# Early q and k on GpSimd's casting queue, a regrouped read of the tail tokens, and fixed operation lists in an attention and channel-mix kernel

## The chip, the core and the metric

The kernel runs on one core of a Trainium2 chip. A core has a matrix engine (TensorE, PE in the profile, with its weight loads as PEld), VectorE (DVE), ScalarE (ACT), GpSimd (POOL), SyncE (SP, which only issues transfers here), and 16 DMA engines that all queues share. SP and ACT have hardware queues (q1 and q10 in the profile); transfers that GpSimd issues go through a software queue (q0) and can change the type on the way. The metric is the time of one execution in microseconds.

## What is computed

`q`, `k` and `v` are [8 batches, 8 heads, 576 tokens, 64]. Everything is given and returned in fp32.

```python
scores = (q @ k^T) / 8 - slope[h] * |i - j|      # slope[h] = 2 ** -(h + 1)
scores where i - j is not in 0..127: -1e9        # causal, window of 128
x = softmax(scores) @ v                          # heads joined: [8, 576, 512]
xk = mu_k * x + (1 - mu_k) * x_prev              # x_prev: x of the token before
xr = mu_r * x + (1 - mu_r) * x_prev
out = sigmoid(xr @ w_r) * ((relu(xk @ w_k) ** 2) @ w_v)   # w_k 512x1024, w_v 1024x512
```

## The kernel before

Attention runs by batch and by pair of heads (g = 0 to 3). q and k are loaded with a cast to bf16, transposed so that the 64 dimensions of the two heads lie on the 128 partitions, and kept in `qk`; the last 64 tokens of a batch (`ts`, `tt`) go a way of their own. Scores of a pair are matmuls into a two-bank PSUM tile `duo` (L729), ACT takes the exponential (L743), VectorE multiplies with a mask that holds bias and window (L756; batch 0 adds the bias on TensorE instead, L716), and AV is a series of 65-column matmuls with a column of ones for the sum (L785). VectorE takes the reciprocal and scales the result into `xu` (L796), which is transposed into `xt`: on TensorE (L823 in batch 0, L840 in batches 1 to 5), or in batches 6 and 7 by a transposing DMA on SP's queue (`out_flip`). VectorE makes `dl` (x minus its predecessor, L883), `xk` and `xr` (L890).

The channel mix works on two batches together in chunks of up to 512 tokens: eight groups of four matmuls with w_k (L994), each followed by ACT's relu (L1001) and a square (L967) into `kk`; per 128 tokens one group of four with w_r (L1012) and ACT's tanh, and two groups of four with the two halves of w_v (L1028), whose sum VectorE multiplies with the gate into `ot` (L1033), which SP writes out. The first chunk of all takes the first 256 tokens of batch 0 (blocks c0 and c1), the second the next 256.

Batch 0 is cut in two parts: part 0 is tokens 0 to 255, part 1 the rest. Part 0's q and k come by hardware queues as fp32 (`first_load`, into `stage`): pairs 0 and 1 by one load each of q and k, cast by VectorE to bf16 and transposed with `ident`; pairs 2 and 3 (FT) by two loads each of q and k with 256 B runs, transposed as fp32 with `id32` in four 128x128 transposes a pair (L1133) and one copy. Part 1 comes by GpSimd's casting queue and is transposed by `qk_quad` in 64x64 blocks (L1089), as is batch 2's `wide_buf`. About 90 matmuls on a zero tile (L690) run whenever TensorE has nothing else at the start.

GpSimd issues its transfers in the order of `LOADS`; there v and V are the v loads of batch 0 (tokens 0 to 255, and the rest with the tail), K and k the halves of w_k, 2 and 3 part 1's q and k of heads 0 to 3 and 4 to 7, t the tail tokens of q and k, a, b and c batch 1's q and k, tail and v, R w_r, W and w the first and second half of w_v. Ahead of them GpSimd makes a distance tile (iota, L440) and cuts it to the window (two selects, L448 and L451).

A planner in Python (`Plan`) makes the order of each engine's instructions when the kernel is built. Each operation is added with its engines, an assumed duration and its dependencies; a simulation then picks, for each engine that is free, the ready operation with the lowest key. The key is the number in `PLACES` that belongs to the operation, with `pe_key` to keep 64-row and 128-row groups together on TensorE and `paced` to hold back transposes of later batches. On the chip each engine executes its list in order and waits by semaphores for data only.

```python
key = (n.place,) + tuple(n.prio)
if rows == 64 and n.rows[0] == 64:
    return (-1e8,) + tuple(key)
```

Of the kernel before, what the change touches and what calls it, by code (L numbers as in the profile page):

```python
# [21 lines left out]
PLACES = [int(x) for x in '''  # L22
# [71 lines left out]
class Plan:  # L94
# [6 lines left out]
    def __init__(self, sizes, pairs, wait=0.0):  # L101
        self.wait = wait
        self.nodes = []
        self.placed = 0
        self.free = {c: set(range(n)) for c, n in sizes.items()}
        self.pairs = pairs
# [1230 lines left out]
```

## Time and profile before

| | us |
|---|---|
| time, median of 3 runs | 232.08 (232.07 to 232.3) |
| time of the profiled execution | 232.05 |
| span of the profiled execution | 230.3 |
| PE busy | 223.5 (97%) |
| DVE busy | 187.7 (82%) |
| ACT busy | 163.1 (71%) |
| POOL busy | 93.9 (41%) |
| L690 warm-up matmuls, 0 to 14 us | 8.05 |

The span runs from the first instruction to the last; 1.75 us of the profiled execution lie around it. Busy time of TensorE is the time with at least one matmul in its pipeline, so 97% is not a share of its peak. GpSimd's busy time is mostly the writing of descriptors for its transfers. Of the 16 DMA engines' time, q0 takes 99.3%, q1 24.0% and q10 1.0% on the page, where several transfers may share an engine, so that shares over 100% occur.

### The profile page before, as it was taken

Reading aid. Unit: us, or ns where it says so; the run is one execution under the profiler, and the core shown is the slowest. Engines: PE = TensorE matmul, PEld = TensorE weight load, DVE = VectorE, ACT = ScalarE, POOL = GpSimd, SP = SyncE. Lnnn points to the kernel's source line nnn. Section 1 sums busy time; section 2 is a strip of 40 time slices with the busy share of each in tenths; the row PEclk is TensorE's granted clock in tenths of the full one; section 3 lists DMA queues with packets and bytes.
Section 4 is the critical chain, followed back from the end, with each engine's and each line's share of the span. In section 5 each row is a group of like instructions: output and inputs, shape, how many; then the busy total and the mean of one; then the engine's idle time right before and its main releaser. Section 6 shows DMA issues by size and latency. Waiting matters only on the chain.

```text
span 230.3 us, 6675 instructions
## 1 busy us (share of the span) xinstructions
PE 223.5 (97%) x2715; PEld 135.2 (59%) x2715; DVE 187.7 (82%) x423; ACT 163.1 (71%) x295; POOL 93.9 (41%) x120
## 2 busy tenths in 40 slices
PE   8999998999999999999999999999999999999994
PEld 8675764765656656455655745545765544545552
DVE  8496998799949998997678997999999979563252
ACT  3769999599989969999797747959476455117421
POOL 8787654579976960991004961700000000000000
PEclk9999999999999999999999999999999999999999
DMA  6999999999999999999643999995230330231032
GB/s 169 183 168 197 189 161 198 193 176 156 189 141 170 160 145 184 96 144 185 141 117 38 173 180 156 131 136 182 78 86 3 137 103 37 89 129 52 3 137 91
DMA packets 121566, 31.11 MB, mean 135 GB/s; under 512 B 108216, under 2 KB 117696, under 8 KB 121536
## 3 DMA queue, kind: packets, MB, share of 16 engines
q0 software_dynamic: 96016, 16.26, 99.3%
q1 hardware_dynamic: 23776, 13.84, 24.0%
q10 hardware_dynamic: 1744, 0.59, 1.0%
q8 instruction: 21, 0.34, 0.6%
q14 instruction: 9, 0.07, 0.1%
HBM read 33.56 MB, written 9.44 MB: 187 GB/s over the span
## 4 chain that ended last, share of the span: by engine, by line
PE 79%; DMA 12%; POOL 4%; issue 2%; DVE 1%; ACT 0%; DVEq 0%; POOLq 0%
PE uno L994 25%; PE uno L1028 25%; PE uno L1012 13%; PE duo L785 7%; PE duo L729 6%; DMA wv_sb<-in_moe_w_v_dram 5%; DMA cb<-in_k_dram 4%; DMA wk_sb<-in_moe_w_k_dram 3%; PE uno L840 3%; POOL vs L503 1%; POOL cb L499 1%; POOL tv L508 1%; DVE ot L1033 1%; PE uno L1089 1%; DVE xr L890 0%
## 5 line engine op out<-in xcount | busy, mean ns | idle before, releaser
L994 PE MATMUL uno<-xk,wk_sb 128*128 128x256 bf16 (+2 forms) x416 | 72.4, 314 | 0.7 <-ACT qk L699 0.4
L1028 PE MATMUL uno<-wv_sb,kk 128*128 128x512 bf16 (+2 forms) x296 | 69.3, 374 | 1.1 <-DMA wv_sb<-in_moe_w_v_dram 1.0
L743 ACT ACTIVATE at<-duo 128x1024 bf16<-128x1024 f32 (+2 forms) x68 | 65.0, 1002 | 5.9 <-PE duo L729 5.5
L1001 ACT ACTIVATE rl<-uno 128x256 bf16<-128x256 f32 (+2 forms) x104 | 48.3, 496 | 25.7 <-PE uno L994 25.1
L994 PEld LDWEIGHTS <-wk_sb 128*128 128x128 bf16 x416 | 38.6, 98 | 23.4 <-issue 0.8
L503 POOL DMA_DIRECT2D vs<-in_v_dram x32 | 28.5, 906 | 40.5 <-PE duo L785 33.7
L1028 PEld LDWEIGHTS <-kk 128*128 128x128 bf16 x296 | 27.2, 98 | 29.7 <-issue 1.5
L756 DVE TENSOR_TENSOR at<-at,mask 128x1024 bf16<-128x1024 bf16 x56 | 37.2, 681 | 7.2 <-ACT at L743 7.2
L967 DVE TENSOR_TENSOR kk<-rl 128x256 bf16<-128x256 bf16 (+2 forms) x96 | 31.3, 337 | 12.5 <-ACT rl L1001 12.0
L1019 ACT ACTIVATE rs<-uno 128x512 bf16<-128x512 f32 x36 | 22.1, 617 | 21.5 <-PE uno L1012 13.2
L1012 PE MATMUL uno<-wr_sb,xr 128*128 128x512 bf16 x144 | 36.9, 380 | 0.0
L1033 DVE SCALAR_TENSOR_TENSOR ot<-rs,uno 128x512 f32<-128x512 bf16 (+2 forms) x37 | 24.2, 662 | 10.7 <-PE uno L1028 8.6
L699 ACT COPY qk<-uno 128x512 bf16<-128x512 bf16 (+1 forms) x41 | 21.8, 600 | 4.7 <-PE uno L1089 3.2
L890 DVE SCALAR_TENSOR_TENSOR xr<-dl,mu_sb,xt 128x576 bf16<-128x576 bf16 (+1 forms) x32 | 24.5, 774 | 0.0
L890 DVE SCALAR_TENSOR_TENSOR xk<-dl,mu_sb,xt 128x576 bf16<-128x576 bf16 (+1 forms) x32 | 24.4, 772 | 0.0
L785 PEld LDWEIGHTS <-at 128*128 128x128 bf16 x576 | 21.2, 98 | 5.0 <-issue 0.4
L796 DVE TENSOR_TENSOR xu<-duo,rc 128x640 bf16<-128x640 f32 x28 | 22.8, 817 | 0.9 <-DMA xt<-xu 0.5
L1012 PEld LDWEIGHTS <-xr 128*128 128x128 bf16 x144 | 13.3, 98 | 13.0
L534 POOL DMA_DIRECT2D cb<-in_k_dram x20 | 17.9, 919 | 4.9 <-DMA vs<-in_v_dram 2.9
L785 PE MATMUL duo<-vs,at 128*128 128x65 bf16 x448 | 19.0, 194 | 0.0
L534 POOL DMA_DIRECT2D cb<-in_q_dram x20 | 17.7, 938 | 0.8 <-PE uno L840 0.7
L699 ACT COPY xt<-uno 128x512 bf16<-128x512 bf16 (+3 forms) x28 | 15.2, 580 | 2.5 <-PE uno L823 1.5
(83 smaller groups left out, 202.8 us busy)
## 6 DMA issues: line engine op xcount, KB each, us to landing
out_dram<-ot SPq DMA_DIRECT2D x30, 256.0 KB, 3.3
vs<-in_v_dram POOLq DMA_DIRECT2D x32, 128.0 KB, 6.6
cb<-in_q_dram POOLq DMA_DIRECT2D x20, 128.0 KB, 6.6
cb<-in_k_dram POOLq DMA_DIRECT2D x20, 128.0 KB, 5.9
out_dram<-ot SPq DMA_DIRECT2D x10, 128.0 KB, 1.8
wk_sb<-in_moe_w_k_dram POOLq DMA_DIRECT2D x2, 512.0 KB, 7.2
cb<-in_q_dram POOLq DMA_DIRECT2D x4, 256.0 KB, 10.2
cb<-in_k_dram POOLq DMA_DIRECT2D x4, 256.0 KB, 10.5
```

Of the source, the lines that this page charges most:

```text
L503: return dma(POOL, 256, issue_t(1024), lambda e: nc.gpsimd.dma_start(out=vs_buf[h.idx][:, j, :, 0:D], in_=v[b, :, 128 * j:128 * j + 128].r ...
L534: return [dma(POOL, 256, issue_t(1024), lambda e, r=r: nc.gpsimd.dma_start(out=cb_buf[h.idx][:, i, r], in_=src[:, :, r]), [g], kind="q") f ...
L699: (nc.scalar.copy if e == ACT else nc.vector.tensor_copy)(out=out, in_=in_)
L743: lambda e, ah=ah, w=w, hp=hp: nc.scalar.activation(out=ah(), in_=two(hp)[:, :, 0:w], func=AF.Exp, scale=float(scale)), (), [hp])
L756: nc.vector.tensor_tensor(out=a, in0=a, in1=m, op=ALU.mult)
L785: nc.tensor.matmul(a[:, hl, t - t0], lhsT=at[:, lo:lo + 128], rhs=vs[:, u, 2 * g + hl, :] if u < NF else tvb[:, 2 * g + hl], start=(u == u ...
L890: lambda e: nc.vector.scalar_tensor_tensor(out=buf[hk.idx][:, g, e0 + c0:e0 + c1], in0=dls(), scalar=mu[:, g:g + 1], in1=xc(1), op0=ALU.mu ...
L967: nc.vector.tensor_tensor(out=out, in0=in_, in1=in_, op=ALU.mult)
L994: nc.tensor.matmul(one(hp)[:, 0:n], lhsT=wk_sb[:, po, 128 * fo:128 * fo + 128], rhs=xk_buf[hx.idx][:, po, c0:c1], start=(po == 0), stop=(p ...
L1001: a = op(ACT, act_t(n), [s], pr, lambda e, hp=hp, hr=hr: nc.scalar.activation(out=rl_buf[hr.idx][:, 0:n], in_=one(hp)[:, 0:n], func=AF.Rel ...
L1012: nc.tensor.matmul(one(hp), lhsT=xr_buf[hx.idx][:, po, 128 * c:128 * c + 128], rhs=wr_sb[:, po], start=(po == 0), stop=(po == NPO - 1))
L1028: nc.tensor.matmul(one(hv)[:, a:b], lhsT=kk_buf[hk.idx][:, fo, o:o + 128], rhs=wv_sb[:, fo, a:b], start=(fo == 0), stop=(fo == NFO - 1))
```

## The change

1. The q and k of batch 0, heads 4 to 7, tokens 0 to 255 are loaded by two transfers of GpSimd's queue (`e` in `LOADS`, into `early_buf` as bf16), issued right after the iota and ahead of all others. The four hardware loads of pairs 2 and 3 and the fp32 transposes go; those pairs take `qk_quad` like part 1, 16 bf16 transposes of 64x64 and two half copies a pair.
2. GpSimd's order at the start is e, v of the first 128 tokens, the two selects, v of the next 128, and then as before.
3. The tail tokens of q and k of batch 0 are read with the group of four tokens as the outer dimension, heads inside; the selection of `ident` columns that transposes them follows.
4. `PLACES`, `pe_key` and `paced` go. `ORDER` gives for PE, ACT and DVE the whole list of operations in order, and each engine takes only the next of its list. The numbers count the operations of these three engines in the order in which the code adds them. On PE: 35 is the transpose of mu, 37 to 126 the warm-up matmuls; 129, 142, 153, 165 the transposes of part 0's pairs; 131, 144, 156, 168 their scores and 133, 146, 158, 170 their AV; 184, 199, 214, 229 the transposes of part 1. 280 and 281 are the two halves of L1028 for block c0 and 285 and 286 for c1; 288 and its like are L994 of the second chunk; 332, 343, 363 and 374 AV of batch 1's pairs 0, 1, 2 and 3, 369 the scores of pair 3; 461, 472, 492 and 503 the transposes of batch 2's pairs; 312 is L1012 of block c2; 1043, 1054, 1065 are AV of batch 7's pairs 1, 2 and 3, and 1092 belongs to the last L994 of the last long chunk.
5. Which of the squares and half copies are ACT's and which VectorE's follows the lists; PE has 425 operations, as before.
6. The reciprocal's buffer is tied to that of `xu`. The number of output tiles that are written as two halves (`n_split`) follows the count of hardware transfers and goes from 5 to 1.

The planner's assumed prices (`COST`, `SKEW` and the like) and the dependencies that hold only in the plan change too; they set no instruction on these three engines.

```diff
-PLACES = [int(x) for x in '''
...
-'''.split()]
+ORDER = {
+    "PE": [int(x) for x in """
+45 43 58 47 57 74 38 53 56 66 73 42 61 67 54 76 46 50 70 59 41 62 60 65 64 71 75 39 69 55 52 51 44 72 48 129 40
+37 49 63 142 77 131 153 144 165 156 35 133 168 146 158 136 78 103 101 91 68 111 88 116 112 113 106 170 149 114
+115 95 79 86 97 85 93 161 100 92 96 107 104 119 80 118 105 123 173 184 94 102 98 124 99 81 125 110 117 199 82
+109 187 229 202 181 257 232 214 189 260 204 87 191 217 90 89 263 219 206 234 122 83 84 194 221 120 126 121 108
+266 236 209 224 272 254 239 355 322 275 324 366 358 283 278 269 327 335 300 317 306 297 338 291 288 280 363 332
+285 281 286 369 461 312 472 343 303 374 503 346 294 459 309 377 475 492 319 314 320 506 315 386 407 495 420 404
+401 395 389 511 392 480 410 569 500 398 415 417 567 464 514 418 422 574 599 423 469 412 425 413 434 483 582 449
...
+983 902 1001 903 1004 1012 1017 1009 1014 1092 1015 1113 1019 1134 1077 1020 1074 1007 1071 1010 1089 1105 1119
+1116 1024 1110 1083 1080 1025 1125 1131 1086 1097 1102 1095 1122 1103 1128 1100 1107 1098 1136 1108 1137 1141
+1139 1142 1144 1145
+""".split()],
+    "ACT": [int(x) for x in """
+10 11 12 130 143 132 155 167 145 157 169 137 150 162 174 185 201 200 188 245 203 258 250 233 190 248 249 205 251
+261 218 247 264 220 262 235 244 195 246 267 210 225 273 268 255 240 356 274 276 325 368 361 359 279 270 367 284
+328 330 307 271 301 298 341 339 292 293 302 299 318 289 372 370 462 474 313 473 304 504 505 348 347 295 296 310
...
+    "DVE": [int(x) for x in """
+0 6 3 2 9 5 1 32 28 27 26 127 128 24 141 140 23 30 25 7 13 16 17 4 14 29 154 31 15 34 166 20 33 8 19 36 134 135
+18 147 159 148 160 171 138 22 172 139 163 186 175 21 176 151 152 164 230 231 183 182 177 259 178 216 215 192 193
+179 180 207 265 208 222 223 196 237 238 252 197 357 323 226 326 198 227 241 228 242 211 256 213 212 243 336 337
...
+}
...
+        self.places = {n: (e, i) for e, ns in ORDER.items() for i, n in enumerate(ns)}
...
         engs = (engs,) if isinstance(engs, str) else engs
+        place = None
+        if engs[0] in ORDER:
+            e, place = self.places[self.placed]
+            assert e in engs
+            engs = (e,)
+            self.placed += 1
...
-    def pe_key(self, n, rows):
-        key = (n.place,) + tuple(n.prio)
-        if rows == 64 and n.rows[0] == 64:
-            return (-1e8,) + tuple(key)
-        if rows == 128 and n.lazy:
-            return (key[0] + self.wait,) + tuple(key[1:])
-        return tuple(key)
...
-                    if e == "PE":
-                        cand.sort(key=lambda n: self.pe_key(n, rows))
+                    if e in turn:
+                        cand = [n for n in cand if n.place == turn[e]]
                     elif e == "FAB":
                         cand.sort(key=lambda n: (n.queue == served, n.base.t0, n.seq))
                     else:
-                        cand.sort(key=lambda n: (n.place,) + tuple(n.prio))
+                        cand.sort(key=lambda n: n.prio)
                     for n in cand:
...
-    LOADS = 'vK23tVkabRcWw'
+    LOADS = 'e0d1K23tVkabRcWw'
-    FT = (2, 3)
-    VCUT = True
-    VDEP = 1
-    KLAST = 1
...
+    early_buf = qx_buf[1].rearrange("p i g s -> p (i g s)")[:, 2048:3072].rearrange(
+        "p (i h r d) -> p i h r d", i=2, r=2, d=D)
...
-                    in_=(q, k)[i][b, :, SM:S].rearrange("h (c r) d -> h c (r d)", r=4)), [g], kind="ts"))
+                    in_=(q, k)[i][b, :, SM:S].rearrange("h (c r) d -> c h (r d)", r=4)), [g], kind="ts"))
...
-    def first_load(i, g, n):
-        hs = (q, k)[i][0, 2 * g:2 * g + 2 * n]
-        eng = KQ if i and g < 2 + KLAST else SPE
+    def first_load(i, g):
+        eng = KQ if i else SPE
         qe = nc.scalar if eng == ACT else nc.sync
-
-        def put(kb, dst, src):
-            return dma(eng, kb, 0.46, lambda e: qe.dma_start(out=dst, in_=src), lat=(0.7, 0.7), kind="first")
-
...
+        return dma(eng, 155, 0.46, lambda e: qe.dma_start(
+            out=stage[:, g, i].rearrange("p (h w) -> p h w", w=128),
+            in_=(q, k)[i][0, 2 * g:2 * g + 2, 0:256].rearrange("h (p r) d -> p h (r d)", p=128)),
+            lat=(1.54, 0.7), kind="first")
+
+    def staged(i, g):
+        return stage[:, g, i].rearrange("p (h r d) -> p h r d", r=2, d=D)
+
+    def early_load(i):
+        return dma(POOL, RUN[2] * 4, issue_t(512), lambda e: nc.gpsimd.dma_start(
+            out=early_buf[:, i].rearrange("p h r d -> p h (r d)"),
+            in_=(q, k)[i][0, 4:8, 0:256].rearrange("h (p r) d -> p h (r d)", p=128)), kind="run2")
...
-    src0 = {}
-    for g, n in ((0, 1), (1, 1), (2, 2)):
-        for i in range(2):
-            x = first_load(i, g, n)
...
+    src0 = {(i, g): [first_load(i, g)] for g in range(2) for i in range(2)}
...
     def load_step(what):
-        if what in "vV":
-            if what == "v" and VCUT:
-                n_w["d"] = pool_op(0.55, emit_cut, [n_ident])
+        if what == "e":
+            for i in range(2):
+                src0[i, 2] = src0[i, 3] = [early_load(i)]
+        elif what == "d":
+            n_w["d"] = pool_op(0.55, emit_cut, [n_ident])
+        elif what in "vV":
             for j in ((0, 1) if what == "v" else (2, 3)):
-                vl[0].append(v_load(0, j, vh[0], [gv[0]] + blank_v + (
-                    src0[1, VDEP - 1] if VDEP and j == 0 else [])))
-                if j == 0 and not VCUT:
-                    n_w["d"] = pool_op(0.55, emit_cut, [n_ident, last[POOL]])
...
+                vl[0].append(v_load(0, j, vh[0], [gv[0]] + blank_v))
             if what == "V":
                 vl[0].append(tv_load(0, vh[0], blank[0:4]))
+        elif what in "01":
+            vl[0].append(v_load(0, int(what), vh[0], [gv[0]] + blank_v))
...
-                        rhs=ident.rearrange("p (g t c) -> p t g c", g=G, t=2)[:, hl],
+                        rhs=ident.rearrange("p (c g t) -> p t g c", g=G, t=2)[:, hl],
...
-    n_hw = 39 + sum(4 if g in FT else 2 for g in range(3)) + 8 * len(XB) + len(XTT) + G * len(XO)
+    n_hw = 39 + 4 + 8 * len(XB) + len(XTT) + G * len(XO)
...
-            f32 = part == 0 and g in FT
-            if f32:
-                cs = src0[0, g] + src0[1, g] + [n_idr]
+            if part == 0 and g < 2:
+                cs = [op(CAST, {ACT: act_t(256, True), DVE: dve_t(256, 2) + 0.08},
+                         src0[i, g], prio + (0,), lambda e, i=i, g=g: copy_any(
+                    e, half_buf[:, 0, i, :, 2 * g:2 * g + 2].rearrange("p r h d -> p h r d"),
+                    staged(i, g))) for i in range(2)]
+                hp = Hold("p1")
+
+                def emit_t(e, g=g, hp=hp):
+                    for i in range(2):
+                        for r in range(2):
+                            nc.tensor.transpose(
+                                one(hp).bitcast(BF16)[:, 256 * i + 128 * r:256 * i + 128 * r + 128],
+                                half_buf[:, 0, i, r, 2 * g:2 * g + 2].rearrange("p h d -> p (h d)"), ident)
+
+                t = op(PE, 0.0565 * 4 * 1.8, cs + [n_ident], prio + (3,), emit_t, [hp, hq0[g]])
+                ys = [op(QK0, {ACT: act_t(512), DVE: dve_t(512)}, [t], prio + (3,),
+                         lambda e, g=g, hp=hp: copy_any(
+                    e, qk_buf[hq0[g].idx][:, :, 0:256].rearrange("p t (c r) -> p t c r", r=2),
+                    one(hp).bitcast(BF16)[:, 0:512].rearrange("p (t r c) -> p t c r", t=2, r=2)),
+                         (), [hp])]
             elif part == 0:
-                cs = []
-                for i in range(2):
-                    cs.append(op(CAST, {ACT: act_t(256, True), DVE: dve_t(256, 2) + 0.08},
-                                 src0[i, g], prio + (0,), lambda e, i=i, g=g: copy_any(
...
+                ys = qk_quad(0, g - 2, 2, lambda: early_buf, src0[0, g] + src0[1, g], prio, 0, hq0[g], True, [])[1]
             else:
-                cs = src1[g // 2]
-            hp = Hold("p1") if part == 0 else None
-
-            def emit_t(e, part=part, g=g, hp=hp, f32=f32):
...
+                ys = qk_quad(0, g, 2, lambda: part_buf, src1[g // 2], prio, 256, hq0[g], False, [])[1]
...
-        t = op(PE, 0.0295 * 2 * NF * m, cl[b] + paced(b, g), prio + (3,), emit, hp + hq, [hc])
+        t = op(PE, 0.0295 * 2 * NF * m, cl[b], prio + (3,), emit, hp + hq, [hc])
...
```

More of the change, by code (lines that the diff above doesn't have):

```diff
@@ L116, in add @@
         n.left = len(edges)
-        n.place = 0
-        if emit is not None and engs[0] in ("PE", "ACT", "DVE"):
-            if prio[0] < 1e11:
-                n.place = PLACES[self.placed]
-                self.placed += 1
-            else:
-                n.place = 1 << 40
+        n.place = place
         for d, w in edges.values():
@@ L410 @@
     last = {}
+    loads = []
     def virtual(key, holds):
@@ L432, in dma @@
         last[queue] = n
+        if queue == POOL:
+            if len(loads) >= 8:
+                loads[-8].succ.append((n, 0.9 + BACK))
+                n.left += 1
+            y = fab(queue, kb / RATE, n, (START, lat[1] + SKEW.get(kind, 0.0)), free, flip)
+            loads.append(y)
+            return y
         return fab(queue, kb / RATE, n, lat, free, flip)
@@ L790, in emit_r @@
         def emit_r(e):
-            nc.vector.reciprocal(out=rc[:, :, 0:nt], in_=a5()[:, :, :, D])
+            nc.vector.reciprocal(out=rc_buf[hx.idx][:, :, 0:nt], in_=a5()[:, :, :, D])
         def emit_x(e):
+            rc = rc_buf[hx.idx]
             out_ = xo().rearrange("p t h d -> p h t d")
@@ L881, in shift @@
         last["xt", b, g] = deps[0]
-        d = op(DVE, dve_t(n, 2), list(deps) + [prev], prio + (1, 0),
+        d = op(DVE, dve_t(n, 2), list(deps) + [prev] + (blank_x if b < 2 else []), prio + (1, 0),
                lambda e: nc.vector.tensor_tensor(
@@ L1126 @@
-            hp = Hold("p1") if part == 0 else None
-            def emit_t(e, part=part, g=g, hp=hp, f32=f32):
-                for i in range(2):
-                    for r in range(2):
-                        nn = 2 * i + r
-                        if f32:
-                            nc.tensor.transpose(one(hp)[:, 128 * nn:128 * nn + 128],
-                                                staged(i, g, r), id32)
-                            continue
-                        nc.tensor.transpose(
-                            one(hp).bitcast(BF16)[:, 128 * nn:128 * nn + 128],
-                            half_buf[:, 0, i, r, 2 * g:2 * g + 2].rearrange("p h d -> p (h d)"),
-                            ident)
```

80 lines of the change are left out of this document (20 added, 60 removed), and 82 rows, old and new, of tables (ORDER, PLACES).

## The prediction

> **What bounds the kernel now.** I read the busy time of each engine in five stretches of the span first, because the limits differ by stage; then TensorE's waits; then the chain that ended last; then the timelines of GpSimd, VectorE and TensorE at the places these name. The columns of the first view are stretch, length, then busy time of PE, PEld, DVE, ACT and POOL, granted clock, DMA share and GB/s.
>
> ```profile
> 14.00:36.60 22.60, 21.73 (x437) 15.09 (x436) 19.94 (x56) 21.65 (x49) 15.43 (x21) 1.00 1.77 180
> 36.60:45.00 8.40, 6.91 (x140) 4.30 (x138) 7.15 (x15) 5.19 (x10) 4.11 (x6) 1.00 1.61 193
> 45.00:204.00 159.00, 159.00 (x1858) 92.37 (x1853) 140.80 (x283) 119.30 (x206) 63.36 (x76) 1.00 1.33 131
> 204.00:230.30 26.30, 22.85 (x137) 12.96 (x135) 10.77 (x26) 9.87 (x21) 0.00 (x0) 1.00 0.22 80
> ```
>
> From 45 to 204 TensorE is never free and its clock is full, so that stage is worth only what its own instructions cost. Idle time lies ahead of 45 and behind 204. The waits say on what:
>
> ```profile
> PE uno L1028 <- DMA wv_sb<-in_moe_w_v_dram: 1.0, 1, 1.0
> PE uno L994 <- ACT qk L699: 0.4, 1, 0.4
> PE uno L994 <- DVE ot L1033: 0.2, 1, 0.2
> ```
>
> The chain, in order of time (start, length, what), and TensorE's timeline show the first of them to be the gate of the whole head:
>
> ```profile
> 4.21 7.44 DMA wk_sb<-in_moe_w_k_dram
> ...
> 16.85 9.14 DMA cb<-in_k_dram
> ...
> 28.21 12.09 DMA wv_sb<-in_moe_w_v_dram
> ...
> 40.34 1.89 PE uno L1028 x8
> ```
>
> ```profile
> 37.76 1.02 PE L1028 MATMUL uno<-wv_sb,kk 128*128 128x512 bf16 x4 [1.01 <-DMA wv_sb<-in_moe_w_v_dram]
> 44.40 0.60 PE L994 MATMUL uno<-xk,wk_sb 128*128 128x256 bf16 x4 [0.43 <-ACT qk L699]
> ```
>
> The chain runs through GpSimd's one DMA queue from 4.2 to 40.3 us: it is full, and the half of w_v that the first L1028 needs lands at 37.7, 1.01 us after TensorE has run out of other work; the second half at 40.3. So for the head two things count: when that queue delivers w_v, and what TensorE has to do meanwhile.
>
> **Part 1, the order ahead of the gate: worth 0 by itself.** Counted in the lists of the diff, the first L1028 group stands at the same place after the warm-up in both orders, behind the same 61 groups. Early q and k of pairs 2 and 3 no longer take 8 fp32 transposes (1.06 us in one row) but 16 bf16 transposes of 64x64 a pair (0.32 us for 16 at 14.00, so 0.64): 0.4 us less. Pairs 2 and 3 may start a little earlier, and the warm-up matmuls, 0.63 us of which still run after 14.0, fill what is left. All of it only makes TensorE reach the gate sooner and wait longer there. If the list made it later instead, the present wait of 1.0 is the cover: it costs nothing up to that.
>
> **Part 2, the gate itself.** Two loads (e) of 512 packets each go onto GpSimd's queue ahead of v; four loads of the hardware queues (2048 packets of 256 B) go away. What they now cost, in packets by queue for 4 to 5 us and for 11 to 13 us:
>
> ```profile
> q1 hardware_dynamic: 481, 0.12, 53.1%
> q10 hardware_dynamic: 403, 0.10, 44.9%
> ```
>
> ```profile
> q0 software_dynamic: 1411, 0.36, 179.8%
> ```
>
> Removed: 2048 packets at 884 in the us are 2.3 us, so that hardware traffic ends near 4.0 and not at 6.3. Added: 1024 packets at 705 a us, 1.45 us. GpSimd's queue now moves 154 packets in 5 to 6 us against 971 in 6 to 7, so its full stream begins in effect at 5.95. In the new order the first issue follows the iota, which ends at 1.18, and not the two affine selects:
>
> ```profile
> 0.84 0.34 POOL L440 IOTA dist<- 128x256 bf16 x1 [0.39 <-POOLq L1321]
> 1.62 0.31 POOL L448 TENSOR_SCALAR_AFFINE_SELECT dist<-dist 128x128 bf16<-128x128 bf16 x1 [0.43 <-DVE ident L444]
> 1.88 0.28 POOL L451 TENSOR_SCALAR_AFFINE_SELECT dist<-dist 128x128 bf16<-128x128 bf16 x1
> 2.22 2.00 POOL L503 DMA_DIRECT2D vs<-in_v_dram  x2
> ```
>
> The first packets came 3.1 us after the first issue (2.22 to 5.3); an idle queue in mid-kernel took 1.6. With 3.1 the first e packet moves at 4.25, the engines are by then free of hardware traffic, e is through at 5.7, and what follows runs 0.25 earlier. That is the value I take, because the row it uses is the same queue at its first use. Ends: with a lag of 1.6 only the hardware traffic ahead limits it, 4.0 + 1.45 = 5.45, and somewhat of e slips in between, 0.7 earlier at most. At the other end v1, now issued behind e, v0 and the selects (end near 5.25), starts 1.95 after its issue ended, as v0 did, at 7.2; e and v0 are through at 5.7 + 0.87, a bubble of 0.6: 0.3 later. Every GpSimd step up to wk's first half is issued later (wk0 by 1.8 less 0.8 for q and k), but from 9 us on GpSimd waits for its own earlier loads ("idle before" of 0.3 to 1.0 from vs and wk rows), so the queue's fill, not the issue, sets the time. The tail tokens (ts) of batch 0 are read token group first: same packets, and near them (13.25 to 14.25) the share of the engines is 164.8% against the 179.8% above. I take the shortfall, 15/180 of 1 us, as regained: 0.1; ends 0 and 0.3. Sum for the gate: 0.35 earlier; ends 0.3 later and 1.0 earlier.
>
> Here one rule speaks against the change, and the row comes first: GpSimd's issues take 0.77 to 0.80 at 4.9 to 8 us, under a busy VectorE, and 0.74 to 0.76 at 14 to 18; the first v issue took 1.12 and its twin 0.89. So a lock costs at most 0.25 an issue. The Trainium skill, page "SBUF — State Buffer", section "SBUF: two separate sides", holds that a GpSimd-queue DMA has its descriptors written by GpSimd, which is shut out for the whole of a VectorE instruction that takes the shared port, while hardware-queue loads are immune. By that rule the move of q and k from hardware queues to GpSimd's exposes them to the start's copies and memsets; no row shows the two at once for these loads. What it would do to the sum is the third rival.
>
> **Part 3, behind the gate.** The new list puts AV of batch 1 (pairs 2 and 0), c1's first half, S of pair 3 and one quad transpose between the halves of L1028 that need w_v's second half, and sets the four quads of batch 2 apart, where before two stood together (64 transposes at 43.26) and L994 waited 0.43 for their ACT copies. So 0.43 and the few hundredths for the second half of w_v are open. Against it: S of batch 1 pair 3 to its AV is now 2.6 us of TensorE work, and the shortest such distance without a wait before is 3.1: 0.5 at worst. Taken: 0.3 gained; ends 0.5 gained, 0.4 lost.
>
> **Part 4, 45 to 204.** The same groups in another order. Summing rows of each engine along the new lists, VectorE's and ACT's work that must be done ahead of each TensorE group is nowhere more than before. Two more changes between 64-row and 128-row groups at 0.1 each are left partly to cover: 0.1 lost; ends 0.3 gained (fewer cold switches elsewhere) and 0.4 lost, about one stall like that at 44.40.
>
> **Part 5, the end.** Before, the last pair's AV ends at 196.4, ten groups of L1028 cover 8.65 us, and then L994 stalls 0.38 in all:
>
> ```profile
> 202.88 0.69 DVE L1033 SCALAR_TENSOR_TENSOR ot<-rs,uno 128x512 f32<-128x512 bf16 x1 [1.94 <-issue]
> 204.22 0.81 DVE L890 SCALAR_TENSOR_TENSOR xk<-dl,mu_sb,xt 128x576 bf16<-128x576 bf16 x1
> 205.68 0.60 PE L994 MATMUL uno<-xk,wk_sb 128*128 128x256 bf16 x4 [0.22 <-DVE ot L1033]
> ```
>
> VectorE stood 1.94 us for an output that was late, with xr and xk behind it. After, again ten groups (8.65) lie between, the chain (reciprocal 0.2, xu 0.8, transposing DMA 1.2 + 2.9, dl 0.4, xr and xk 1.5, some queueing 1.0) is 8.0, and the list puts xk ahead of the late output. Taken: 0.3 gained; ends 0.4 gained and, if the transposing DMA is late by a us, 0.3 lost. Fewer output tiles are written in halves (n_split 5 to 1) and tiles ahead of the last are long out by the end: 0. Casts, copies and squares moved between VectorE and ACT change no TensorE wait named here: 0, covered by the leads of part 4; cost without cover 0.3 an operation.
>
> **Sum.** The profiled execution took 232.05 (span 230.3, 1.75 around it), 0.03 under the median 232.08. 232.05 - 0.35 (gate) - 0.3 (behind it) + 0.1 (mid) - 0.3 (end) = 231.2.
>
> **Rivals.** (A, the other side) The queue is late: nothing is saved at the start and all behind e is late. Place: the first packets of q0. Break-even is at 4.5 (5.95 less e's 1.45); past 5.1 the 0.6 of parts 3 and 5 is eaten too, and there it decides. First packets at 5.3 as before are 0.8 late, with v1's bubble of 0.6 it is 1.4: 232.05 + 1.4 - 0.5 = 232.95. For it: 5.3 is what the row shows; against: the issue is 1.0 earlier. (B) The strict order stalls TensorE: AV of pair 3 by 0.5 and two stalls of 0.4 between 45 and 204, with the gate earlier by 0.35 and the end unchanged gives 232.05 + 0.5 + 0.8 - 0.35 - 0.4 = 232.6. For it: leads are near those that already stall; against: 159.00 of 159.00 busy. (C) Gain hidden: w_v lands as before and the fillers, and the list's end, only move their waits; 232.0. (D) Lag of 1.6 and no stall left: 232.05 - 0.7 - 0.5 - 0.4 = 230.45. (E) GpSimd shut out at the start: e0, e1 and v0 each wait 0.25 as the first v issue did, 0.7 in all, the gate 0.35 later instead of earlier: 231.9. By the page named above this would be the rule, and no run here shows it yet.
>
> **Chances.** Forecast 0.46, D 0.08, C 0.12, E 0.05, A 0.18, B 0.11. Against no change measured to 0.2% (0.46 us, about what this kernel's runs can tell): faster 0.54, same 0.17, slower 0.29. The likeliest alone spans 230.8 to 231.6; the range reaches to D and A: 230.5 to 233.0.
>
> **What would show it.** Gate: the first L1028 starts at 37.4 with a longer wait, w_v still its releaser; right for A if it starts past 38.2. Start: first q0 packets near 4.25, none from the hardware queues after 4.2. Behind: no 0.43 at L994 after the quads, no wait at AV of batch 1. End: no wait of L994 on VectorE after the last L1028 run. It is wrong if new waits appear from 45 to 204 or the first packets stay at 5.3.

## The result and the profile after

The changed kernel takes 234.58 us (median of 6 executions, 233.26 to 235.43) against 232.07 for the kernel before: ratio 1.0102, 95% interval 1.0081 to 1.0123. It is slower by 2.5 us where 0.9 faster was forecast, and lies outside the range. Its executions spread over 2.2 us, those of the kernel before over 0.5 here; beside the later runs the kernel before spreads over 1.8 to 3.1 too, so this difference in spread says little. The profiled execution took 234.76, with a span of 233.0.

Busy time by stretch of the changed kernel (columns as in the prediction):

```profile
14.00:36.60 22.60, 21.37 (x419) 14.89 (x421) 18.36 (x49) 20.06 (x45) 15.22 (x20) 1.00 1.73 174
36.60:45.00 8.40, 8.17 (x120) 4.89 (x121) 7.16 (x14) 6.34 (x15) 4.88 (x6) 1.00 1.50 193
45.00:204.00 159.00, 154.75 (x1851) 92.82 (x1878) 142.67 (x285) 121.06 (x209) 63.55 (x76) 1.00 1.37 131
```

The third line looks as if 4.25 us of idle time had come up between 45 and 204. Most of it is not real: 1878 weight loads stand beside 1851 matmuls, so 27 matmul records are missing, and each leaves a gap in the busy time. The waits of TensorE from 45 to 56, below, show what is real, and the timelines give its place and the start of the first w_v group (L1000 is the old L1028, L820 the old L840, L966 the old L994):

```profile
PE uno L820 <- issue: 1.4, 1, 1.4
PE uno L820 <- ACT rl L973: 0.2, 1, 0.2
PE uno L1061 <- DVE qk L679: 0.2, 1, 0.2
```

```profile
38.41 1.04 PE L1000 MATMUL uno<-wv_sb,kk 128*128 128x512 bf16 x4
...
50.00 0.59 PE L820 MATMUL uno<-ident,xu 64*128 64x64 bf16 x10
52.00 0.32 PE L820 MATMUL uno<-ident,xu 64*128 64x64 bf16 x10 [1.41 <-issue]
```

Two things stand out. The first w_v group starts at 38.41 instead of 37.76, 0.65 late. And TensorE stops for 1.41 us in the middle of one group of 20 transposes; "issue" means that nothing the profile shows released it. The quad wait of 0.43 that the prediction wanted to remove is gone, with 0.16 and 0.24 in its place, and so is the stall of L994 behind the last L1028 run. The chain, in order of time, still goes through GpSimd's queue; w_v's first half lands at 28.70 + 9.66 = 38.36:

```profile
5.35 7.40 DMA wk_sb<-in_moe_w_k_dram
...
16.89 9.44 DMA cb<-in_q_dram
...
28.70 9.66 DMA wv_sb<-in_moe_w_v_dram
```

GpSimd's timeline, start and length of each issue:

```profile
1.34 0.91 POOL L555 DMA_DIRECT2D qx<-in_q_dram  x1 [0.16 <-issue]
2.24 0.77 POOL L555 DMA_DIRECT2D qx<-in_k_dram  x1
2.98 0.91 POOL L499 DMA_DIRECT2D vs<-in_v_dram  x1
3.87 0.33 POOL L446 TENSOR_SCALAR_AFFINE_SELECT dist<-dist 128x128 bf16<-128x128 bf16 x1
...
5.35 0.77 POOL L540 DMA_DIRECT2D wk_sb<-in_moe_w_k_dram  x1
...
13.04 0.89 POOL L499 DMA_DIRECT2D vs<-in_v_dram  x1 [2.00 <-DMA wk_sb<-in_moe_w_k_dram]
```

The load of w_k's first half goes out at 5.35 (4.21 before), and the wait for its landing, ahead of v's fourth block, is 2.00 us (1.02 before; 1.61 in a second trace of the changed kernel). The packets of the software queue (packets, MB, share of 16 engines) for 4 to 5, 7.5 to 8.25 and 16.5 to 17.5 us of the changed kernel:

```profile
q0 software_dynamic: 552, 0.14, 146.1%
```

```profile
q0 software_dynamic: 249, 0.07, 99.1%
```

```profile
q0 software_dynamic: 284, 0.07, 152.0%
```

In 4 to 5 us the queue moves 552 packets, with the hardware queues out of the way (16 packets in the same us); in 5 to 6 it moves 786. The prediction took 705 for e, from 11 to 13. And there are two holes: 0.07 MB where the kernel before moved 0.13 (7.5 to 8.25, a share of 99.1% against 158.1%) and 0.16 (16.5 to 17.5, 152.0% against 202.0%).

### The profile page after: what moved, and what is told of

The parts are those of the page before. It is cut to its first block, busy times and chain, and to the rows that moved or that the text cites. A ratio compares the mean times of both kernels' runs of the same rounds, so it can differ in the third digit from the quotient of the medians.

```text
span 233.0 us, 6676 instructions
## 1 busy us (share of the span) xinstructions
PE 222.4 (95%) x2705; PEld 136.3 (58%) x2739; DVE 188.2 (81%) x420; ACT 164.2 (70%) x300; POOL 94.8 (41%) x122
## 4 chain that ended last, share of the span: by engine, by line
PE 36%; issue 19%; DMA 18%; POOL 16%; SPq 4%; ACT 4%; DVE 1%; DVEq 0%; POOLq 0%; ACTq 0%
PE uno L1000 13%; PE uno L966 12%; DMA cb<-in_q_dram 7%; POOL cb L530 7%; PE uno L984 6%; POOL vs L499 4%; DMA wv_sb<-in_moe_w_v_dram 4%; SPq L534 4%; PE duo L764 3%; DMA wk_sb<-in_moe_w_k_dram 3%; DMA ts<-in_k_dram 2%; DMA xt<-xu 2%; POOL ts L520 2%; ACT at L723 2%; POOL tv L504 1%
## 5 line engine op out<-in xcount | busy, mean ns | idle before, releaser
L966 PE MATMUL uno<-xk,wk_sb 128*128 128x256 bf16 (+2 forms) x410 | 73.4, 313 | 0.6
L1000 PE MATMUL uno<-wv_sb,kk 128*128 128x512 bf16 (+2 forms) x279 | 67.6, 373 | 1.5 <-issue 0.8
L966 PEld LDWEIGHTS <-wk_sb 128*128 128x128 bf16 x416 | 38.9, 98 | 24.7 <-issue 0.4
L1000 PEld LDWEIGHTS <-kk 128*128 128x128 bf16 x296 | 27.2, 98 | 27.9 <-DMA wv_sb<-in_moe_w_v_dram 0.4
L947 DVE TENSOR_TENSOR kk<-rl 128x256 bf16<-128x256 bf16 (+2 forms) x91 | 28.7, 339 | 9.2 <-ACT rl L973 8.9
L984 PE MATMUL uno<-wr_sb,xr 128*128 128x512 bf16 x133 | 35.5, 380 | 0.5
```

What stands on the lines that cost most here:

```text
L947: nc.vector.tensor_tensor(out=out, in0=in_, in1=in_, op=ALU.mult)
L966: nc.tensor.matmul(one(hp)[:, 0:n], lhsT=wk_sb[:, po, 128 * fo:128 * fo + 128], rhs=xk_buf[hx.idx][:, po, c0:c1], start=(po == 0), stop=(p ...
L984: nc.tensor.matmul(one(hp), lhsT=xr_buf[hx.idx][:, po, 128 * c:128 * c + 128], rhs=wr_sb[:, po], start=(po == 0), stop=(po == NPO - 1))
L1000: nc.tensor.matmul(one(hv)[:, a:b], lhsT=kk_buf[hk.idx][:, fo, o:o + 128], rhs=wv_sb[:, fo, a:b], start=(fo == 0), stop=(fo == NFO - 1))
```

## The experiments

Two theories stood. One: the two loads e at the head of GpSimd's queue make everything on that queue late, w_v too. Two: the new lists themselves cost time, above all the 1.41 at L820, either for data or because TensorE waited for its own code. "Fixed lists of before" below means the operation order that the planner of before had made, written into `ORDER`. The kernel before was timed again beside each run, with medians of 232.03 to 232.15, so times of different runs are set side by side.

### The two halves of the change, apart

First the lists of the change with the loads of before:

```diff
-    LOADS = 'e0d1K23tVkabRcWw'
+    LOADS = 'dvK23tVkabRcWw'
     # pairs 2 and 3 again by 4 hardware loads and fp32 transposes, ts read head first
```

> The changed kernel with the loads of before: early q and k of pairs 2 and 3 by the hardware queues and transposed as fp32, GpSimd's order selects, v0, v1, w_k, the old read of the tail tokens; the new operation lists stay (VectorE makes the fp32 identity earlier, the pairs' copies are still two). Theory of two causes, loads 0.65 us (first L1000 at 38.41 against 37.76) and order the rest: the first w_v group starts at 37.7 to 37.9, the wait of 1.4 near 52 is still there, time about 234.58 - 0.65 = 233.9. If the loads are the whole loss: 232.1. If the order is the whole loss: 234.6.

Measured: 234.67 (234.03 to 235.39), ratio 1.0104 (1.0060 to 1.0149). This looks like "the order is the whole loss", but the trace says otherwise. The first w_v group starts at 40.25, later than in any other run, although w_v's first half has landed at 38.23. TensorE itself comes late: the new lists put pairs 2 and 3 early, where the hardware loads deliver them late (their fp32 transposes wait 1.9 us in two waits). In this execution TensorE's granted clock also falls, to 0.65 in 10 to 12 us and 0.50 in 12 to 14, where four matmuls of L724 take 0.50 us instead of 0.34; the other three executions have a mean clock of 0.999 or 1.000. In this kernel the wait at L820 is gone, and another of the same kind is in the middle of a group of 32 transposes (0.53 at 32.40, "issue"). New lists and old loads do not fit together, and this run does not separate the halves. The next does:

```diff
 ORDER = {
-    "PE": [... the lists of the change ...]
+    "PE": [... fixed lists of before ...]
```

> The changed kernel with the operation lists that the planner of before made (the copies of pairs 2 and 3 as two neighbours); loads and tail-token read are the new ones. Theory of two causes: the first w_v group starts near 38.4, no wait of over 1 us between 45 and 55, the quad wait of 0.43 is back, time 232.07 + 0.65 = 232.7. If the loads are the whole loss: 234.6. If the order is: 232.1, or less if the regrouped tail read helps.

Measured: 233.25 (232.22 to 234.15), ratio 1.0049 (1.0028 to 1.0070); first w_v group at 38.15 in its fastest execution, no wait over 0.43 behind it, the quad wait of 0.43 back. So the loads cost over 1 us without the new lists, and the lists 1.3 more: two causes. The trace is of an execution 1.03 faster than the median, so what the ordinary one waits for is not in it; in it w_v's first half lands at 37.56, and TensorE starts on it 0.59 later, when its own work ahead is done.

### What e costs

```diff
-    LOADS = 'e0d1K23tVkabRcWw'
+    LOADS = '0d1K23tVkabRcWw'
-    ys = qk_quad(0, g - 2, 2, lambda: early_buf, ...)[1]
+    ys = qk_quad(0, g - 2, 2, lambda: half_buf[:, 0]..., cast0[g - 2], ...)[1]
```

> The changed kernel without the two early loads e: pairs 2 and 3 of part 0 take the cast q and k of pairs 0 and 1 instead (wrong values for heads 4 to 7, first 256 tokens; same instructions on all other engines). Theory that e's two issues and 1024 packets ahead of all else are what makes w_v late: GpSimd issues w_k's first half 1.7 us earlier, its wait for that half is 1.0 or less again, first w_v group at 37.6 to 37.8 instead of 38.4, time down by 0.65 to 1.2 (233.4 to 233.9), and the spread between executions shrinks. If the late w_v comes from the new operation lists: no change, 234.6.

This kernel leaves out the two loads e, and pairs 2 and 3 of part 0 work on pairs 0 and 1's q and k instead. Measured: 233.04 (232.18 to 235.77), ratio 1.0054 (1.0015 to 1.0094), 1.54 less than with e. The first w_v group starts at 36.61, 0.10 after w_v's first half has landed. GpSimd's timeline of this kernel:

```profile
1.62 1.03 POOL L499 DMA_DIRECT2D vs<-in_v_dram  x1 [0.43 <-DVE ident L442]
...
4.12 0.76 POOL L540 DMA_DIRECT2D wk_sb<-in_moe_w_k_dram  x1
...
11.51 0.89 POOL L499 DMA_DIRECT2D vs<-in_v_dram  x1 [1.71 <-DMA wk_sb<-in_moe_w_k_dram]
```

Each of these issues is 1.2 to 1.5 us earlier. The wait for w_k's half is still 1.71, not the 1.0 expected, so e does not make it. The spread over all executions did not shrink; but four of the ten had a mean granted clock of 0.990 to 0.992 and took 234.71 to 235.77, and the six at 0.998 to 1.000 took 232.18 to 233.05, median 232.59. What lowered the clock is not traced. The same on the fixed lists of before:

> The lists of before with the new loads but without the two loads e (pairs 2 and 3 of part 0 take the cast q and k of pairs 0 and 1: wrong values for heads 4 to 7, first 256 tokens). With the new lists e cost 1.5 (234.58 to 233.04). Theory that e delays the whole GpSimd queue by about its own 1.45 us whatever the order: 233.25 - 1.2 = about 232.0, of which the gate can give back no more than its wait. Rival, e costs much only because the new lists need part 0 early: at most 0.3 less than 233.25.

Measured: 231.70 (231.15 to 232.00), ratio 0.9980 (0.9963 to 0.9996): 1.55 less than with e, and no execution of the one overlaps the other. By the medians e costs the same under both lists, about the 1.45 that the prediction had priced for its packets: it is paid in full. The traces of the old lists with and without e do not show the 1.55: their executions took 232.22 and 232.00, the fastest of the one kernel and the slowest of the other, and w_v's first half lands at 37.56 with e and 37.33 without.

Its removal also shows what the rest of the new loads gain, the hardware traffic taken away. In the time it is nothing: 231.70 against 231.48 for the same lists with the old loads (below). In the traces it is less than credited, but not nothing: w_v's first half lands at 37.33 here, and with the old loads at 37.71 (before), 38.20 and 37.75 (two runs below). Behind the gate this trace has a wait of 0.49 that those three lack; it is of the kind that is taken up below. In this kernel w_k's half is issued at 3.82, 0.39 before the kernel before, and lands at 12.00, 0.35 after it:

```profile
3.82 8.18 DMA wk_sb<-in_moe_w_k_dram
```

That says little: with one and the same order of the old loads this load takes 7.44, 8.23 and 7.13 us in the three traces.

### Whether the wait for w_k's half is the hole

```diff
-    LOADS = 'e0d1K23tVkabRcWw'
+    LOADS = 'e0d123KtVkabRcWw'
```

> The changed kernel with GpSimd's load of the first half of w_k (512 KB) moved behind part 1's q and k. GpSimd holds back a load until the eighth one before it has landed; in the changed kernel v's third block waits 2.0 us for that half of w_k, and at 16.5 to 17.5 its queue then moves half of what it moves before and after. Theory that this hole is what makes w_v late: no wait for w_k ahead of v's third block, no hole at 16.5, w_v earlier by 0.5 to 0.7, time 233.9 to 234.1. Rival, w_v is late because of the bytes and packets of e alone: same 38.4 and 234.6.

Measured: 235.05 (233.40 to 235.90), ratio 1.0107 (1.0049 to 1.0164): no gain, and w_v is later, the first group at 39.41. The wait has only moved, to a later load, and grown:

```profile
16.67 0.74 POOL L495 DMA_DIRECT2D cb<-in_k_dram  x1 [2.51 <-DMA wk_sb<-in_moe_w_k_dram]
```

So that wait at that place is not what makes w_v late. Nor does its size go with the loads: with the old loads it is 1.02, 2.11 and 0.92 in three traces, with the new loads and old lists 1.14, without e there 2.78. With lists and loads of before the same move:

> The operation lists and the loads of before, written with fixed lists (the copies of pairs 2 and 3 halved), and the load of w_k's first half moved behind part 1's q and k as in the run beside it. If GpSimd's wait for that half is a hole in the queue here too (1.0 us at 10.9 to 11.9): w_v 0.2 to 0.5 earlier and time 231.6 to 231.9. If there is no hole here: 232.0.

Measured: 231.32 (230.78 to 232.74), ratio 0.9963 (0.9938 to 0.9988), the fastest kernel of this study. But what it shares with before counts too:

> The operation lists and the loads of before, written with fixed lists and the copies of pairs 2 and 3 halved: what the run with w_k's first half moved has in common with before. If that move is what made it faster, this one is within 0.2% of before (232.1); if the halved copies or the buffers that the fixed lists take did, it is at 231.3 too.

Measured: 231.48 (230.84 to 232.45), ratio 0.9984 (0.9967 to 1.0002). Writing the old order as fixed lists is worth up to 0.6 by the medians, not established by the interval; the move of w_k on top of it at most 0.2, not established either.

### The read of the tail tokens

```diff
-    in_=(q, k)[i][b, :, SM:S].rearrange("h (c r) d -> c h (r d)", r=4)
+    in_=(q, k)[i][b, :, SM:S].rearrange("h (c r) d -> h c (r d)", r=4)
```

> The changed kernel with the tail tokens of batch 0 read head first, as before. If the regrouped read spreads the transfer over more of the DMA engines and that is worth what the prediction took (0.1, at most 0.3): w_v later by 0.1 to 0.3, time 234.7 to 234.9. If it is worth nothing: 234.6. If it was a loss: below 234.5.

Measured: 235.41 (234.38 to 236.19), ratio 1.0133 (1.0088 to 1.0178); by the medians the regrouped read is worth 0.6 to 0.8 in the changed kernel, with intervals that overlap widely, and two of the four executions here had a granted clock of 0.991 and 0.993 (235.66 and 236.19; the others 234.38 and 235.17). Part 1's transposes wait 1.79 for their load there (0.47 and 0.2 in the changed kernel's two traces), which fits a queue that is slowed by it, but one trace does not make a size. Where the gate has slack, nothing is left:

> Lists and loads of before with fixed lists, w_k's first half behind part 1's q and k, and of the change only the regrouped read of the tail tokens. If that read spreads the two transfers over all engines and this reaches w_v: 0.1 to 0.3 below the run without it (231.0 to 231.2). If it doesn't reach TensorE: 231.3.

Measured: 231.40 (231.03 to 232.25), ratio 0.9981 (0.9968 to 0.9993), no better than without the regrouped read.

### The wait of 1.41: data or code

The instruction queue of the page has 21 packets, for 2739 weight loads and as many matmuls, so one piece of 16 KB holds about 256 of TensorE's instructions, 128 weight loads with their matmuls:

```profile
q8 instruction: 21, 0.34, 0.6%
```

One of the pieces was fetched just ahead of the 1.41: between 49.6 and 50.6 (first line below, with 6.0% of 16 engine-us, 0.96 us). From 50.6 to 52.0, while TensorE stands, there is only data traffic (second fence).

```profile
q8 instruction: 1, 0.02, 6.0%
```

```profile
q0 software_dynamic: 1693, 0.21, 252.1%
```

If the wait is for code, moving every instruction in the code must move it to another operation:

```diff
+    SKIP = (... the last 24 warm-up matmuls of the list ...)
-        plan.add(PE, ..., emit_warm, (), [h_wm])
+        plan.add(PE, ..., (lambda e: None) if i + 37 in SKIP else emit_warm, (), [h_wm])
```

> The changed kernel with the last 24 of the 90 warm-up matmuls left out (they compute nothing that is used), so that every later TensorE instruction stands 48 places earlier in TensorE's code. Theory that the 1.41 us at 52.0 is a wait for TensorE's own code, which comes in pieces of 16 KB (128 weight loads with their matmuls): the long wait leaves the middle of the L820 group; a wait, if there is one, comes at the 863rd weight load again, 24 weight loads later in the program; time 233.2 without it, up to 234.6 with it. Rival, a wait for data or a buffer of that L820 group: it stays at the eleventh matmul of the group with 1.4, time 234.6.

Measured: 234.99 (233.02 to 236.29), ratio 1.0136 (1.0087 to 1.0185). In its profiled execution, its fastest, the L820 group runs without a wait, and no other takes its place. The median did not fall. Two of the four executions had a granted clock of 0.993 (234.87 and 236.29); what the fourth, 235.11 at 1.000, waited for is not seen. With 60 left out:

> The changed kernel with the last 60 of the 90 warm-up matmuls left out, so that the pieces of TensorE's code are cut 60 weight loads later in the program, through the middle of the dense stretch at 45 to 50 us. Theory of the code wait: no wait of over 0.5 us for nothing that the profile shows, from the first w_v group on; if one is left it stands at a weight load whose number is 94 plus a multiple of 128 (478, 606, 734, 862). Time 233.2 to 233.6, where only w_v is late. Rival, waits for data: the L820 group keeps its 1.4, 234.6.

Measured: 234.31 (233.27 to 236.31), ratio 1.0112 (1.0071 to 1.0153). Six of the eight executions had a granted clock of 0.983 to 0.993 and took 233.76 to 236.31; the two at 1.000 took 233.27 and 233.68, about what was expected. So leaving out warm-up matmuls may cost clock as well as move the code, and only runs at full clock tell of the code. The L820 group has no wait, and one appears in the middle of the scores of batch 1's first pair:

```profile
32.67 0.39 PE L711 MATMUL duo<-qk 64*128 64x256 bf16 x3
33.86 0.38 PE L711 MATMUL duo<-qk 64*128 64x256 bf16 x4 [0.81 <-issue]
```

Where such waits stand is best counted in weight loads. From the start of the span to just before the end of the wait, in the changed kernel, in its second trace, without e, and in the run with 60 fewer (the number after x):

```profile
0.00:51.90 51.90, 33.57 (x862) 1.00 1.62 174
```

```profile
0.00:50.90 50.90, 33.35 (x862) 1.00 1.64 176
```

```profile
0.00:49.40 49.40, 32.84 (x862) 1.00 1.60 176
```

```profile
0.00:33.70 33.70, 18.68 (x479) 1.00 1.58 163
```

862 each time, at 51.9, 50.9 or 49.4 us; also with the old tail read, with w_k moved, and with the old lists without e, where the first matmul behind weight load 862 is another one (0.49 us there). 479 is three pieces of 128 earlier, but for one, and the wait at 32.40 of the new lists with the old loads also ends behind weight load 479. The second trace of the changed kernel:

> The changed kernel again, for a second trace of it. Theory: first w_v group at 38.2 to 38.7 once more; a wait for nothing that the profile shows at weight load 862 (or 478, 606, 734) of 0.3 to 1.6 us, its size following from when the 16 KB of code landed; time 234 to 235. If the 1.41 of the first trace was an accident of one execution, no such wait is there, and the time is then 1.4 lower.

Measured: 234.80 (233.72 to 236.39), ratio 1.0128 (1.0092 to 1.0164); first w_v group at 37.76, the wait again at weight load 862 and 1.00 long:

```profile
50.95 0.32 PE L820 MATMUL uno<-ident,xu 64*128 64x64 bf16 x10 [1.00 <-issue]
```

Last, the test from the other side: the old lists and old loads, cut so that a piece ends in their dense stretch.

> The old lists and old loads with fixed lists (231.48 on its own) and the last 24 warm-up matmuls left out; nothing else differs. By the theory of the code wait the pieces of code are now cut so that the 128 weight loads up to number 734 are consumed in 3.1 us (quads and AV of 42 to 46 us), where a refill took 4 to 7 us from its start to use: a wait for nothing that the profile shows, 1.5 to 3 us, right at weight load 734 (or 862), and a time of 232.8 to 234. By the rival, that the waits at weight load 862 belong to the new lists' data: no such wait, 231.5.

Measured: 232.77 (231.91 to 233.88), ratio 1.0035 (1.0010 to 1.0059), 1.29 over the same kernel with all warm-up matmuls (231.48), though all that was done is to leave out instructions. The clock is not it: two of the ten executions had 0.993, and the other eight, at 0.999 or 1.000, have a median of 232.67. Its timeline has two waits that the other does not have, in the middle of a group of 32 and of one of 20:

```profile
29.94 0.44 PE L1078 MATMUL uno<-ident,cb 64*64 64x64 bf16 x31
30.97 0.19 PE L1078 MATMUL uno<-ident,cb 64*64 64x64 bf16 x1 [0.59 <-issue]
...
45.51 0.43 PE L837 MATMUL uno<-ident,xu 64*128 64x64 bf16 x17
46.58 0.23 PE L837 MATMUL uno<-ident,xu 64*128 64x64 bf16 x3 [0.64 <-issue]
```

The weight loads up to 30.9 and 46.5 us there:

```profile
0.00:30.90 30.90, 20.29 (x479) 1.00 1.54 179
0.00:46.50 46.50, 29.57 (x734) 1.00 1.61 183
```

479 and 734 (862 less 128), as the theory of the code wait wants; 0.64 long, not the 1.5 to 3 expected. Shifted the other way nothing happens:

> The same with 16 of the warm-up matmuls issued twice, so that the cuts come 16 weight loads earlier in the program and the quickest piece lasts 5.8 us instead of 5.5. By the theory of the code wait: no wait, 231.3 to 231.6. If more warm-up matmuls matter for themselves (they take up to 0.9 us ahead of the first w_v group, under its wait): also 231.5. It tells whether a shift as such costs anything.

Measured: 231.69 (231.29 to 232.75), ratio 0.9976 (0.9944 to 1.0007), no such wait. That TensorE waits for its code at these places is shown: the waits keep to the count of instructions and move, go or come when instructions far ahead are left out.

When the wait comes is a matter of two times. In the ten waits of these traces the fetch of the next piece starts 1.9 to 4.5 us after TensorE has entered the piece before, takes about 1 us, and TensorE goes on 1.3 to 2.0 us after its end; it stands if its instructions last less than that. In the changed kernel the fetch starts 4.33 after weight load 734, and the 128 weight loads last 5.1: it stands 1.41. With 24 warm-up matmuls fewer the fetch starts 2.73 after, and 5.3 us of weight loads are just enough. With the old lists without e even 6.2 us are not, because the fetch starts 4.46 after (wait 0.49). Why the fetch starts late is open.

The page "Runtime: NRT & Kernel Launch" of the Trainium skill, section "Instruction fetch mechanics", says that code is refilled in blocks of 16 KiB, 256 instructions, and that crossing a boundary is mostly hidden. The size agrees with these traces (the waits at weight loads 479, 734 and 862 lie 255 and 128 apart); that it is hidden does not hold at these places, where TensorE stands 0.49 to 1.55 us.

### The sum of it

| us, median | old loads | new loads | new loads without e |
|---|---|---|---|
| old lists | 231.48 | 233.25 | 231.70 |
| new lists | 234.67 (does not fit) | 234.58 | 233.04 |

By these medians e costs 1.55 and 1.54, the lists 1.33 and 1.34, and the rest of the new loads 0.2. That the two add up so closely is luck: with the six executions at full clock alone (232.59 instead of 233.04) e costs 2.0 under the new lists, and the lists 0.9 without e. That both e and the lists cost something holds either way.

## Why the prediction was wrong

**The gate (0.35 earlier taken; 0.65 later in the first trace, 0.0 in the second; e costs 1.55 in time).** This is the larger of the two errors. The failing step is "from 9 us on GpSimd waits for its own earlier loads (...), so the queue's fill, not the issue, sets the time", and with it the credit of 1.7 us of earlier start against 1.45 of e. e's cost was met almost to the tenth in time. The credit was mis-sized: without e w_v's first half lands 0.4 to 0.9 earlier than with the old loads under the old lists, and nothing of that is left in the time (231.70 against 231.48).

The packets of the software queue show where the start was lost. Up to 7 us the sum held: the queue had moved 2381 packets against 1125 before, 232 more than e's own 1024, which at 705 a us is 0.33 us (0.25 was taken). By 9 us it is 3305 against 2304, 23 fewer than e's 1024; in the second trace the lead falls from 179 to 29. So the start was lost ahead of the stretch that the failing sentence speaks of. Between the two the queue moves 924 packets at a share of 137.4%, where the kernel before moved 1179 at 164.9%, so it was not full. Without e under the old lists it is 1052 packets ahead at 7 us and 331 at 8.25, at a share of 112.8%. That GpSimd's issues, 1.1 us later behind e, set the pace in this stretch is argued from these rows, not tested. The hole behind v1 and w_k's late issue, which stood among the bounds with 0.6, is part of it (0.07 MB against 0.13 in 0.75 us) and should have been taken. What happens from 9 us to w_v is open: its first half lands at 38.36 in the first trace, and at 37.71 and 37.56, where it was before, in the second and in that of the old lists with e, whose executions were 1.0 to 1.1 faster than their medians.

**Rival A (slower, 232.95, 0.18)** came nearest, partly by luck. The new loads do cost 1.8 under the old lists (233.25 against 231.48), but its 1.4 was put together from first packets at 5.3, 0.8 late, and 0.6 for v1's bubble. The first packets moved before 4, so the head start was there and did not last.

**The order ahead of the gate (0 taken).** Right in kind while w_v is the gate: in the traces of the changed kernel and without e the first w_v group starts within 0.1 us of the landing of w_v's first half (38.36, 37.71 and 36.51 with the new lists, 37.33 with the old).

**Behind the gate (0.3 gained taken).** The quad wait went as forecast and left 0.4 of smaller ones; AV of batch 1's pair 3 has no wait. The second failing step is here: the wait for code, 1.41 and 1.00 in two traces of the changed kernel, is a term that the prediction put at nothing. It weighed lists by what engines wait for from each other and not by how many instructions a us they ask for. In the new lists the 128 weight loads ahead of number 862 take 5.1 us (45.3 to 50.4), in the lists of before 6.3 (45.2 to 51.4), and between the entry into a piece and the use of the next there lay 6.7 us in the changed kernel (45.3 to 52.0). From the first w_v group to the end of the span the second trace has 194.1 us (231.9 - 37.76), the old lists with the same loads 192.25 (230.4 - 38.15). 1.0 of the difference is the code wait. The other 0.9 is there in every trace: less the code waits, this stretch lasts 193.1 to 193.5 in the eight traces with the new lists and 192.1 to 192.5 in the eight with the old. About 0.7 of it is busy time of TensorE for the same 2124 matmuls (189.2 in the second trace, 188.5 in the old lists with 16 more warm-ups), so the order itself costs TensorE time, against 0.1 taken for "the same groups in another order"; which neighbours cost it is open.

**45 to 204 (0.1 lost taken)**: apart from the code wait no wait above 0.25 is there. **The end (0.3 gained taken)**: the stall behind the last L1028 run is gone, as forecast; its size was not measured by itself. **The tail read (0.1)**: not settled, between 0 and 0.8.

**Rival E**, VectorE shutting out GpSimd: e's two issues take 0.91 and 0.77, v's 0.91 and 0.90, the old first v issue 1.12. The rule of the Trainium skill, page "SBUF — State Buffer", section "SBUF: two separate sides", is not seen at work here.

**The chances.** Slower had 0.29. No rival joined the causes that made it so: A alone would have ended at 232.95, and with the code wait and the list's own cost behind it the time is 1.6 above that.

## What to carry to other kernels

Before loads are put at the head of a queue that carries everything else, price them in full at its far end, and credit an earlier start only as far as the later issues keep the queue fed. Where an engine runs many short instructions, count them as a resource: here the refill of TensorE's code took 4.2 to 6.9 us from entering one piece to using the next wherever TensorE had to wait, and 256 instructions that last about 5 us could be over before it. Then leaving out instructions far ahead moves the wait to another operation or creates one. A wait that ends in the middle of one group, with no releaser, at the same count of instructions in several kernels, points to code; leaving out a few instructions ahead tests it. And look at the granted clock of every execution before two medians are compared.

## What the runs showed of the hardware that was not expected

A warm-up matmul that computes nothing changes the time by where it puts the cuts in the code: with the old lists and loads 24 fewer cost 1.29 us (231.48 to 232.77), 16 more at most 0.2. A piece of code that starts to arrive at 49.6 to 50.6, 0.96 us long, lets TensorE go on at 52.0, so about 1.4 us pass between its last byte and its first use (1.3 to 2.0 in ten such waits). And the landing of w_k's first 512 KB, 6.5 to 8.2 us after its issue in these runs, holds GpSimd's queue for 0.9 to 2.8 us in nearly every trace, wherever that load stands.
